# First transfers of the last stage rearranged in a forward and backward kernel of a recurrent-memory transformer block

## Chip, cores, metric

One core of one Trainium2 chip. The metric is the device time of one execution in microseconds (us), as the median of several executions. The kernel before took 3069.97 us (three runs, 3061.94 to 3073.0). In the profile lines PE is TensorE (PEld its weight loads), DVE VectorE, ACT ScalarE, POOL GpSimd and SP SyncE; a "queue" is the list of DMAs that one of these engines issues.

## The reference, cut to what matters

The forward pass is a block with two branches on a layer norm: an attention branch that goes through the sequence in 64 segments of 32 rows and carries 8 memory rows from each segment to the next, and a squared-ReLU MLP. The kernel computes the output and the gradients of ten arguments (`jax.vjp`).

```python
for s in range(n_seg):                       # 64 segments
    h = concat([mem, xs[s]])                 # 8 memory rows + 32 rows, D = 512
    q, k, v = h @ Wq, h @ Wk, h @ Wv         # 32 heads of 128
    p = softmax(mask(q @ k.T * scale))
    o = (p @ v) @ Wo
    mem = o[:M]; outs.append(o[M:])
out = x + concat(outs) + (relu(xn @ w1 + b1)**2 @ w2 + b2)
```

Two stretches matter here. The *recurrence* is the backward pass through the 64 steps, last step first, in 16 blocks of four steps. The *last stage* then computes the weight gradients of Wq, Wk, Wv and Wo, as 16 columns of 160 matmuls each, and the input gradient, 128 rows per column ("input rows").

## The kernel before

The recurrence is written as a list of named operations per step; the kernel plays the list for each block. `L.` marks operations of a block, and `+` or `-` moves an operation by one block or step. The third and fourth row, cut:

```python
B_ORDER = (
    ...
    "... o1te s0 vea L.gs d10 vp1 vla ..."           # third row: L.gs of the block before
    "klb1- o0mm o1mm L.vst o0ev ... vtr ... L.ldt+ ldq- vla d10 L.qtr ... kp0 ldk- ..."   # fourth row
...
o["gs"]  = lambda: dma(S_GM[:, :, b*P:(b+1)*P], gts[b][:])   # store the block's GT
o["ldk"] = lambda: left_of_step(dma, tile_of("kLs", ...), b, j, 1)   # four loads of b_kLs
# dma = SyncE's queue, pdma = GpSimd's queue, nc.scalar.dma_start = ScalarE's queue
```

GT is the gradient that one step hands to the next; DVE writes its last part at the end of the third row. S_GM is its copy in memory, which the last stage reads transposed, as GOc. `qtr` is a DMA transpose, and `ldk` loads b_kLs, which PE reads in the fourth row.

The last stage:

```python
def rows_of(i, g, blocks, left_):            # one column: all in one tile
    t_ = pool.tile([P, RC_ALL, CW], ...)
    q = pdma if i < 2 else dma
    ...
with tc.manual_schedule():
    loads(0)                                 # column 0: GpSimd's queue, 5 MB
    slot_side(GOc, S_GM, gflat)              # 4 DMA transposes + 4 loads, SyncE
    loads(1)                                 # column 1: GpSimd's queue, 5 MB
    slot_side(side, S_HT, S_XN[:])           # HNc, the other operand for Wq, Wk and Wv
for i, (t, g) in enumerate(COLS):            # 16 columns
    loads(i + 2)
    ...                                      # 160 matmuls, evictions, stores on GpSimd's queue
    input_rows(NB - 1 - i)                   # loads, transposes and arithmetic of 128 rows
```

## Time and profile before

| stretch of the profiled execution | us |
|---|---|
| recurrence: end of the first reduction of GT to end of the last | 918.3 |
| from there to the end of the last matmul of the backward pass (ps_m): "last block" | 21.0 |
| first hole: to the first matmul of the last stage | 54.8 |
| last stage: first to last matmul of a weight gradient | 577.6 |
| tail: to the end | 12.4 |

The engines by stretch show start:end, length, then busy us and instructions of PE, PEld, DVE, ACT and POOL, granted clock of PE, DMA share, GB/s.

```profile
1475.71:2394.03 918.32, 829.20 (x21088) 423.37 (x21088) 447.80 (x1278) 332.09 (x945) 352.49 (x683) 0.99 0.70 177
2394.03:2415.04 21.01, 19.20 (x428) 11.04 (x424) 10.65 (x30) 5.81 (x16) 5.93 (x9) 1.00 0.78 261
2469.82:3047.45 577.63, 563.27 (x2622) 258.81 (x2623) 52.78 (x91) 79.79 (x157) 155.35 (x252) 0.98 0.91 188
```

PE is busy for 829 of 918 us in the recurrence: whatever makes PE wait there lengthens the whole. The waits and the chain in the two holes are shown in the prediction.

### The profile page before, as it was taken

How to read it: one execution, taken by the hardware profiler on the slowest of the kernel's cores; microseconds unless marked ns; L12 is line 12 of the kernel's file. 1: busy time of each engine (PE TensorE's matmuls, PEld its weight loads, DVE VectorE, ACT ScalarE, POOL GpSimd, SP SyncE). 2: the span in 40 equal slices, each digit the busy share in tenths (PEclk: the TensorE clock that was granted, in tenths of full speed). 3: DMA queues.
4: the chain of work that ended last, by engine and by line, in shares of the span. 5: the costliest groups of instructions: out<-in, count | busy, mean ns of one | idle time of the engine just before them, and what ended most of it. 6: DMA issues, size and time to landing. Idle time of an engine off the chain costs nothing. (4 is left out here: it accounts for less than half of the span.)

```text
span 3059.8 us, 109712 instructions
## 1 busy us (share of the span) xinstructions
PE 2705.4 (88%) x48600; PEld 1386.8 (45%) x48600; DVE 1319.5 (43%) x3581; ACT 994.7 (33%) x2306; POOL 658.0 (22%) x1264
## 2 busy tenths in 40 slices
PE   8997899999999886877799899998989559999998
PEld 4453444444444444446444444444444224444443
DVE  5452566666666664334345444544545201100010
ACT  2422444444444444323333333333333101111111
POOL 0000000000000000113343433434343213322222
PEclk9998999999999998999999999999999879999999
DMA  9548375766767767777577676776777899898991
GB/s 257 185 146 250 101 188 161 189 181 172 190 168 182 165 157 192 229 230 220 149 173 174 190 187 164 177 203 169 176 200 175 238 192 217 194 211 207 204 207 39
DMA packets 794559, 566.78 MB, mean 185 GB/s; under 512 B 579409, under 2 KB 681570, under 8 KB 790754
## 3 DMA queue, kind: packets, MB, share of 16 engines
q1 hardware_dynamic: 748322, 430.47, 58.8%
q0 software_dynamic: 40528, 126.53, 13.5%
q8 instruction: 381, 6.24, 0.9%
q10 hardware_dynamic: 5232, 2.75, 0.4%
q14 instruction: 96, 0.79, 0.1%
HBM read 193.61 MB, written 238.56 MB: 141 GB/s over the span
## 5 line engine op out<-in xcount | busy, mean ns | idle before, releaser
L1505 PE MATMUL ps_gw<-gn,HNc 128*128 128x512 bf16 x1920 | 416.4, 379 | 0.0
L1505 PEld LDWEIGHTS <-HNc 128*128 128x128 bf16 x1920 | 187.8, 98 | 223.9
L374 ACT CAST f_N<-ps_proj 128x512 bf16<-128x512 f32 x320 | 185.9, 581 | 243.9 <-PE ps_proj L392 223.4
L1476 ACT CAST wt<-ps_gw 128x512 bf16<-128x512 f32 x128 | 74.4, 586 | 503.5 <-PE ps_gw L1505 474.4
L392 PEld LDWEIGHTS <-X 128*32 128x32 bf16 x6144 | 153.3, 97 | 161.3 <-DVE X L482 13.9
L835 POOL COPY kM<-f_kT 128x256 bf16<-128x256 bf16 x64 | 25.6, 401 | 786.7 <-DVE f_kT L377 594.9
L1459 DVE TENSOR_TENSOR gx<-ps_rows,gb 128x512 f32<-128x512 f32 x16 | 11.1, 692 | 420.5 <-PE ps_rows L1457 418.2
L1505 PE MATMUL ps_gw<-GOc,gn 128*128 128x512 bf16 x640 | 142.2, 385 | 54.8 <-DMA GOc<-S_GM 54.8
L460 PE MATMUL ps_gR<-Wk,gk 128*32 128x512 bf16 x2048 | 146.7, 386 | 19.4 <-ACT gk L374 12.9
L392 PE MATMUL ps_proj<-Wk,X 128*32 128x512 bf16 x2048 | 135.4, 384 | 12.6 <-DVE X L482 6.9
L460 PE MATMUL ps_gR<-Wq,gq 128*32 128x512 bf16 x2048 | 141.6, 382 | 1.2 <-issue 1.2
L374 ACT CAST gk<-b_pp 128x256 bf16<-128x256 f32 x192 | 68.8, 377 | 208.3 <-PE b_pp L547 146.6
L1477 POOL DMA_DIRECT2D out_dram<-wt x128 | 69.2, 541 | 309.5 <-ACT wt L1476 309.4
L1239 POOL COPY PD<-b_P 32x320 bf16<-32x320 bf16 x256 | 114.9, 449 | 95.3 <-PE b_pp L1292 64.4
L460 PE MATMUL ps_gR<-Wv,gv 128*32 128x512 bf16 x2048 | 133.4, 379 | 0.3 <-issue 0.3
L392 PE MATMUL ps_proj<-Wo,GT 128*32 128x512 bf16 x2048 | 123.9, 384 | 7.9 <-POOL GT L1203 6.7
L392 PE MATMUL ps_proj<-Wq,X 128*32 128x512 bf16 x2048 | 128.7, 382 | 0.0
L460 PE MATMUL ps_R<-Wo,OT 128*32 128x512 bf16 x2048 | 126.4, 388 | 0.0
L469 PE MATMUL ps_sum<-identF,R 128*128 128x128 f32 x512 | 102.4, 295 | 24.6 <-ACT R L374 18.4
L392 PE MATMUL ps_proj<-Wv,X 128*32 128x512 bf16 x2048 | 124.1, 378 | 0.0
L1505 PEld LDWEIGHTS <-gn 128*128 128x128 bf16 x640 | 63.4, 99 | 132.3 <-issue 59.6
L374 ACT CAST gON<-ps_proj 128x512 bf16<-128x512 f32 x128 | 74.9, 585 | 143.2 <-PE ps_proj L392 141.5
(260 smaller groups left out, 5128.0 us busy)
## 6 DMA issues: line engine op xcount, KB each, us to landing
S_A<-f_N SPq DMA_DIRECT2D x64, 512.0 KB
out_dram<-wt POOLq DMA_DIRECT2D x142, 128.0 KB, 4.6
S_A<-f_N SPq DMA_DIRECT2D x64, 256.0 KB
S_GB<-gv SPq DMA_DIRECT2D x32, 512.0 KB
S_GB<-gq SPq DMA_DIRECT2D x32, 512.0 KB
S_GB<-gk SPq DMA_DIRECT2D x32, 512.0 KB
b_kN<-S_A POOLq DMA_DIRECT2D x63, 256.0 KB, 5.0
b_qN<-S_A POOLq DMA_DIRECT2D x63, 256.0 KB, 5.4
```

Of the source, the lines that this page charges most:

```text
L374: nc.scalar.copy(out, in_)
L392: nc.tensor.matmul(o, lhsT=hT[:, dc, :], rhs=x, start=(dc == 0), stop=(dc == DC - 1), tile_position=(0, 32 * g))
L460: nc.tensor.matmul(o, lhsT=XT(k, g), rhs=x, start=(first and k == 4 * h), stop=(last and k == 4 * h + 3), tile_position=(0, 32 * g))
L469: nc.tensor.transpose(st["T"][:, c * P:(c + 1) * P], R4()[:, c * P:(c + 1) * P], identF[:])
L835: o["km"] = lambda: nc.gpsimd.tensor_copy(B_["kM"][:, :, :, lc], T["kT"][:, :, :, 0:M])
L1239: nc.gpsimd.tensor_copy(PD[32 * g:32 * g + 32, g], C["P"][32 * g:32 * g + 32, :, 0:L])
L1459: nc.vector.tensor_tensor(out=gx[:], in0=ps[:], in1=gb[:], op=ALU.add)
L1476: nc.scalar.copy(wt[:], ps[:])
L1477: pdma(dst, wt[:])
L1505: nc.tensor.matmul(ps[:], lhsT=l(rc), rhs=r(rc), start=(n == 0), stop=(n == RC_ALL - 1))
```

## The change

The intent is to close the hole between recurrence and last stage, and the smaller one behind the first column. GOc's transposes should not share the DMA engines with 10 MB of columns, the stores that they wait for should leave early and from another queue, and the input rows should be there when PE wants them. The core of the diff, shortened:

```diff
-  third row:  "... s0 vea L.gs d10 vp1 ..."       fourth row: "klb1- o0mm o1mm L.vst o0ev ..."
+  third row:  "... s0 vea d10 vp1 ..."            fourth row: "klb1- o0mm o1mm L.gs+ L.vst o0ev ..."
...
+  q = nc.scalar.dma_start if b == 0 and n != "v" and x else dma      # last block's S_GB stores
-  o["sl"] = lambda: dma(S_XGL[b], ...)
+  o["sl"] = lambda: (dma if b > 1 else nc.scalar.dma_start)(S_XGL[b], ...)
-  o["sx"] = lambda: dma(S_XG[b], ...)             # also: the store of gm
+  o["sx"] = lambda: (dma if b > 0 else nc.scalar.dma_start)(S_XG[b], ...)
...
   # a column is now two tiles, gn (16 blocks) and gl (left rows), loaded in parts
-  loads(0)
+  first, second = columns(0), columns(1)
+  for f in first[:2]: f(pdma)                     # 2 MB of column 0 on GpSimd's queue
   slot_side(GOc, S_GM, gflat)
-  loads(1)
+  for f in first[2:] + second: f(dma)             # the rest on SyncE's queue, behind GOc
   slot_side(side, S_HT, S_XN[:])
+  loads(2)
+  load_rows(NB - 1)                               # input rows, one column ahead, on GpSimd's queue
...
-  input_rows(NB - 1 - i)                          # after the last job of a column
+  if k == 3 or i == 0: input_rows(NB - 1 - i)     # after the fourth job
```

The first hunk is written for the last block (the stage's reader waits for that store), but the list is played for every block. A detail that no comment tells: the number `x` of a half is not bound when the store is made, so by the time the four S_GB stores of q and k in the last block are issued it is 2 (a later loop in the same function uses the name again), and all four go on ScalarE's queue.

## The prediction

> **What bounds the kernel now.** I read the page first, then the chain of waits over the last quarter, then the waits of TensorE (PE) there, then the engines by stretch, and last the timeline of single hand-overs. PE is busy 88% of the span; the page's row of slices has one hole (two slices of 5 tenths, 2371 to 2524 us), where the recurrent backward pass ends and the last stage (the weight gradients) begins. The stretches, with PE's busy time as first figure after the length:
>
> ```profile
> 2340.00:2415.00 75.00, 68.56 (x1700) 35.83 (x1692) 37.38 (x107) 24.86 (x73) 28.15 (x52) 1.00 0.73 206
> 2415.00:2470.00 55.00, 0.22 (x2) 0.14 (x2) 1.56 (x5) 0.00 (x0) 4.47 (x7) 0.54 0.93 251
> 2506.00:2521.00 15.00, 0.64 (x4) 0.32 (x3) 0.23 (x1) 3.13 (x6) 8.14 (x16) 0.67 1.11 234
> 2557.00:3048.00 491.00, 490.88 (x2305) 226.43 (x2302) 48.91 (x84) 71.56 (x141) 135.36 (x217) 1.00 0.89 185
> ```
>
> Before 2415 and after 2557 PE is full; between lie two holes, of 55 and 15 us. The waits of PE name them:
>
> ```profile
> PE ps_gw L1505 <- DMA GOc<-S_GM: 54.8, 1, 54.8
> PE ps_rows L1457 <- DVE XT L1448: 14.4, 1, 14.4
> ```
>
> The chain of waits (start, length, what) tells what fills the first:
>
> ```profile
> 2409.55 20.80 DMA gNat<-b_gkL
> 2431.05 16.92 DMA gNat<-b_gvL
> 2448.03 1.31 SPq L1423
> 2449.38 1.31 SPq L1423
> 2451.05 4.79 DMA GOc<-S_GM
> 2456.00 3.06 DMA gNat<-b_gqL
> 2459.07 2.40 SPq L1408
> 2462.04 2.73 SPq L1408
> 2464.82 4.76 DMA GOc<-S_GM
> ```
>
> These are DMA transposes, issued from ScalarE (gNat) and SyncE (GOc), one stream after the other. The same size of transpose (256 KB) takes 20.80 and 16.92 us, then 3.06. During the slow two, GpSimd's queue moves both first columns of gn, 10.5 MB. The packets tell why: in most 5 us slices from 2415 to 2445 the two queues start nearly the same number of packets (440 and 439 from 2435), 4 KB ones of about 160 ns against 256 B ones of about 20 ns. A 256 KB transpose is 64 small packets on each of 16 engines: 64 x 20 ns = 1.3 us alone, 64 x (20 + 160 to 225) ns = 12 to 16 us beside the big ones.
>
> The hand-over that will matter later is one step of the recurrence, SyncE's queue against DVE and PE:
>
> ```profile
> 2320.70 0.56 SPq L1148 DMA_DIRECT2D S_GM<-GT  x1
> 2324.34 0.62 SPq L1190 DMA_DIRECT2D S_GL<-gNat  x1
> 2329.66 1.30 SPq L1247 DMA_TRANSPOSE b_vl<-S_A  x1
> 2331.68 1.24 SPq L1188 DMA_TRANSPOSE gNat<-b_gqL  x1
> 2333.01 1.47 SPq L566 DMA_DIRECT2D b_kLs<-S_NL  x4
> 2335.75 0.29 DVE L482 TENSOR_REDUCE GT<-ps_sum 128x32 bf16<-128x128 f32 x1 [0.53 <-PE ps_sum L469]
> ```
>
> PE reads b_kLs at 2342.09, 6.04 us after that reduction ended. By the landing marks in the trace b_kLs landed at 2340.4: 1.7 us to spare. Over the 14 full blocks the time from reduction to use is 6.03 to 6.21 us and the spare time 0.05 to 3.0 us.
>
> **What the Trainium skill says.** "DMA: Bandwidth & Descriptors", section "Queues, rings and completion order", says that each DMA engine round-robins between queues by the packet; the counts above agree. Its section "Silent corruption: two transposing streams in flight at once" says that transposes of ScalarE and SyncE must wait for each other's completion; the chain shows those waits (SyncE goes on at 2448.03, when gNat<-b_gvL has landed). "Advanced Engine Details and Errata", section "Sequencer Loop", says that control work is done as it is read, so a DMA issue that waits holds up what stands behind it in that queue; the trace agrees: SyncE issues nothing from 2415.4 to 2448.0. "TensorE: Matmul & The Clock Gate", section "What's actually happening", says that an idle PE starts at half clock; here the clock is 0.54 in the hole and the first 160 matmuls take 36.53 us against 34.53.
>
> **The change, part by part.** I built the changed kernel and resolved each wait to the instruction that ends it.
>
> 1. *First hole.* Of the first column only two loads (2 MB) go on GpSimd's queue, and only Wo's last reader, at about 2396, holds them. The rest of column 0 and all of column 1 stand on SyncE behind GOc. ScalarE's queue gets four S_GB stores and S_XG ahead of its transposes. Expected, on the clock of before (ScalarE free at 2409.4): five issues of 0.33 to 0.65 us, so the k transpose issues at 2412.4. The stores are 2048 packets of 1 KB, 128 per engine x 46 ns = 5.9 us, S_XG 0.7, from 2411.5 to 2418.1; the transpose 1.3 us behind them and its landing: 2420.5. The v transpose takes 3.1 (as gNat<-b_gqL did): 2423.6. GOc's first 4.4: 2428. The q transpose 3.1: 2431. GOc's other three 10.5 (2459.07 to 2469.6 before), and 3 us for the input rows of two blocks, 1.6 MB of big packets that GpSimd now loads just then: 2444.5. Gain 2469.8 - 2444.5 = **25.3 us**. Column 0's second half and its left rows (3 MB) are issued by 2450 and needed 14 and 28 us after the start; column 1 (5.2 MB) needs about 15 us at the mean 354 GB/s of 2410 to 2440 and is due 36 us after the start. Both arrive in time. gn for column 2 follows at about 1.6 us a transpose and should be there 5 to 10 us early; I allow **1 us** of loss.
> 2. *Second hole.* The input rows are loaded a job ahead, so their transposes follow the first job at once. From the end of the first job (2506.35) to the second's first matmul (2521.59) were 15.2 us; now an eviction and 1.1 us of ps_rows, about 1.5. Gain **13.7**, and **1.7** more, because PE does not fall to half clock (36.27 against 34.53 us).
> 3. *Tail.* Input rows are worked off in mid-column, so after the last matmul only an eviction and one store remain, not the row arithmetic. The last store was issued at 3056.55; now at 3048.41, as the last weight store was. Gain **8.1**.
>
> ```profile
> 3048.41 0.54 POOL L1477 DMA_DIRECT2D out_dram<-wt  x1 [3.78 <-ACT wt L1476]
> 3056.55 0.58 POOL L1472 DMA_DIRECT2D out_dram<-gi  x1 [2.88 <-issue]
> ```
>
> 4. *The store of S_GM in every block.* Moving it to the head of the block's own last step is meant for the last block, but all 16 get it. Where it stood before it waited for nothing on DVE; now it waits for the reduction of 2336.04, and the S_GL store, the b_vl transpose, b_vTL, the q transpose and the four b_kLs stand behind it. SyncE then runs: S_GM to 2336.7, S_GL to 2337.1, b_vl to 2338.4, b_vTL to 2339.0, the q transpose once S_GL has landed (2339.4) to 2340.7, the last b_kLs issued at 2341.9. A landing takes 2.1 to 2.6 us from there: about 2344.3. PE wants it at 2342.1. So PE stands still about 2.2 us per block. PE has hardly any other idle time here (eleven holes over 0.9 us in 900 us), so nothing absorbs it: 14 x 2.2 = **31 us lost**. In the last block the 2 MB of column 0 (from 2398, 32 big packets per engine) lie beside the q transpose, whose landing and that of b_kLs behind it slip by some 4 us: **6 us**.
>
> Sum: -25.3 - 13.7 - 1.7 - 8.1 = -48.8; +31 + 6 + 1 = +38. From 3070: 3059; as the S_GM term is the softest and some overlap with today's spare time is possible, I say 3057.
>
> **Rivals.** (a) The S_GM move is harmless: then 3070 - 48 = 3022. For it: before, b_kLs waits in rings crowded by GpSimd's b_kN, b_P and b_qN (4 to 6 us to land), and later it would have free rings. Against: the issues alone end at 2341.9 and the spare time is 1.7. (b) It costs 4 us a block, if b_vl and its copy on GpSimd (2340.06 before) become late too, or the rings stay crowded: 3085. (c) The first hole closes further, because the transposes find an empty DMA: at most to some 20 us, for five serial transposes and landings remain; 3048 with the S_GM loss, 3013 without. (d) A new wait opens in the last stage, at columns 1 to 3, since 8 MB and then 36 transposes must follow in one queue while PE runs 36 us a column; SyncE needed 37 us for one column at 2506 beside other traffic. That would give back 5 to 15 us: up to 3072.
>
> **Range and chances.** The gap terms are sure to some 6 us, the block term to 14 x 1.5 = 21 us, the new waits to 8: about 23 together, so an 8-in-10 range of 3028 to 3086. Faster by over 2% is below 3008.6: it needs rival (a) and (c) together and more, 3%. Slower by over 2% is above 3131: over 7 us a block, 3%.
>
> **What would show it.** Right, if PE's wait for GOc<-S_GM is 25 to 33 us and gNat<-b_gkL takes 8 to 10; if the wait of ps_rows is gone and the last store follows the last eviction; if PE waits for b_kLs in each block's last step by about 2 us and the recurrence from 1560 to its end is some 35 us longer. Wrong, if the recurrence has kept its length (then near 3022), if TensorE waits for gn at columns 1 to 3, or if GOc's transposes still find a crowded DMA.

## The result, and the profile after

The changed kernel took **3101.97 us** (four runs, 3096.11 to 3106.75), the kernel before 3068.68 (four runs). The ratio is 1.011, with a 95% interval of 1.0081 to 1.0138. The sign is sure, and 3102 lies above the predicted range (3028 to 3086).

| stretch | before | after | difference | predicted |
|---|---|---|---|---|
| recurrence | 918.3 | 984.5 | +66.2 | +31 |
| last block | 21.0 | 33.8 | +12.8 | +6 |
| first hole | 54.8 | 33.0 | -21.8 | -25.3 |
| last stage (second hole, clock, new waits) | 577.6 | 568.4 | -9.2 | -14.4 |
| tail | 12.4 | 9.7 | -2.7 | -8.1 |
| all before the recurrence | 1475.7 | 1474.6 | -1.1 | 0 |
| span of the profiled execution | 3059.8 | 3104.0 | +44.2 | -10.8 |

The three stretches shown of before, in the changed kernel:

```profile
1474.55:2459.00 984.45, 864.27 (x21088) 434.96 (x21088) 448.34 (x1278) 332.35 (x945) 353.62 (x683) 0.96 0.64 165
2459.00:2492.85 33.85, 21.23 (x429) 11.70 (x424) 10.66 (x30) 5.82 (x16) 1.51 (x2) 0.85 0.69 180
2525.89:3094.32 568.43, 561.18 (x2573) 258.78 (x2624) 55.79 (x94) 79.96 (x159) 151.87 (x243) 0.99 0.98 204
```

The recurrence issues the same 21088 PE instructions. Its idle time (length less PE's busy time) went from 89.1 to 120.2 us, +31.1. That is what the prediction had, though the match to 0.1 us is luck: the waits for b_kLs alone came to 35.6 us in 14 blocks (1.45 to 3.25 us each, but for a few short ones behind them), and other idle time fell by 4.5. But PE's *busy* time grew as well, by 35.1 us, for the same instructions, and the clock went from 0.99 to 0.96.

The waits of PE from the recurrence on (us in total, times, longest):

```profile
PE b_pp L547 <- DMA b_kLs<-S_NL: 46.4, 18, 10.8
PE ps_gw L1528 <- DMA GOc<-S_GM: 33.0, 1, 33.0
```

The first line did not exist before; it holds the blocks' waits and the last block's of 10.8 us. The second is the first hole (54.8 before), and the 14.4 us wait of ps_rows, the second hole, is gone. How a block's wait comes about can be read from SyncE's queue in one block (start, us, operation); the reduction of GT ends at 2266.82:

```profile
2266.85 0.55 SPq L1148 DMA_DIRECT2D S_GM<-GT  x1
2267.45 0.63 SPq L1192 DMA_DIRECT2D S_GL<-gNat  x1
2268.18 1.33 SPq L1249 DMA_TRANSPOSE b_vl<-S_A  x1
2270.38 1.24 SPq L1190 DMA_TRANSPOSE gNat<-b_gqL  x1
2271.71 3.32 SPq L566 DMA_DIRECT2D b_kLs<-S_NL  x4
```

Everything stands behind the store, which stands behind the reduction. In the kernel before (the prediction shows such a block) the last b_kLs load was issued about 1.6 us *before* the reduction ended; here it is issued 8 us after. Between the reduction's end and PE's use lay 6.03 to 6.21 us before and 7.6 to 9.4 us after. What PE does in that block:

```profile
2264.03 1.04 PE L460 MATMUL ps_gR<-Wq,gq 128*32 128x512 bf16 x16
...
2275.97 0.75 PE L547 MATMUL b_pp<-gST,b_kLs 8*128 8x32 bf16 x4 [3.04 <-DMA b_kLs<-S_NL]
...
2276.82 1.90 PE L460 MATMUL ps_gR<-Wv,gv 128*32 128x512 bf16 x16
2278.50 1.92 PE L460 MATMUL ps_gR<-Wk,gk 128*32 128x512 bf16 x16
```

This is the line that the prediction lacks. Sixteen matmuls of the same shape take 1.04 us ahead of the wait and 1.90 and 1.92 us behind it. The trace's clock records agree: in the recurrence the clock was 0.5 for 13.7 us in 3 stretches before and for 81.9 us in 16 stretches after. Each stretch lasts 3.41 or 6.83 us, and but for two of the 16 each begins within 2 us of the end of a wait for b_kLs. At half clock 68.2 us more cost at most 68.2 x (1 - 0.5) = 34 us. PE's busy time leaves 24 to 27 us for it. The matmuls of ps_gR alone are busy for 402.2 instead of 378.0 us (+24.2). Or, from the whole: 35.1 less about 8, because the first group of four late b_kLs matmuls takes 0.75 instead of 0.20 us (each of the four starts some 0.18 us after the one before), in 14 blocks; that is not the clock, since in e4 below such a group takes 0.73 us where the clock is full.

In the last block it is the loads of column 0:

```profile
2461.28 1.51 POOL L1424 DMA_DIRECT2D gn<-S_ON  x2 [5.87 <-PE ps_proj L392]
2463.49 1.45 SPq L566 DMA_DIRECT2D b_kLs<-S_NL  x4
2475.86 0.86 PE L547 MATMUL b_pp<-gST,b_kLs 8*128 8x32 bf16 x4 [10.75 <-DMA b_kLs<-S_NL]
```

GpSimd's two loads of 1 MB are issued just ahead of b_kLs, and PE's use of b_kLs is 12.4 us after its issue instead of the 4.3 of the block shown above. Later in the same block, from 2480 to 2487 us, no queue has anything to move.

The first hole shrank, but its end is slower than it could be (chain of waits; the last line is SyncE issuing GOc's transposes):

```profile
2491.96 5.09 DMA gNat<-b_gkL
2501.05 4.81 DMA GOc<-S_GM
2505.88 3.05 DMA gNat<-b_gqL
2513.99 4.86 SPq L1410
```

gNat<-b_gkL went from 20.80 to 5.09 us, as intended (the prediction had 8 to 10). From the second GOc transpose (2508.95) to the first matmul (2525.89) it takes 16.9 us, where the prediction had 10.5 and 3: GpSimd loads the input rows of two blocks just then, at 2512 to 2520. New waits for gn at column 2 came to 4.2 us. The tail is at the end of the next section.

### The profile page after: what moved, and what is told of

The parts are those of the page before. It is cut to its first block, busy times and chain, and to the rows that moved or that the text cites. A ratio compares the mean times of both kernels' runs of the same rounds, so it can differ in the third digit from the quotient of the medians.

```text
span 3104.0 us, 109562 instructions
## 1 busy us (share of the span) xinstructions
PE 2732.7 (88%) x48451; PEld 1400.1 (45%) x48600; DVE 1320.4 (43%) x3581; ACT 995.1 (32%) x2306; POOL 650.1 (21%) x1250
## 5 line engine op out<-in xcount | busy, mean ns | idle before, releaser
L1528 PE MATMUL ps_gw<-gn,HNc 128*128 128x512 bf16 x1510 | 346.9, 380 | 5.5 <-DMA gn<-S_GB 4.2
L460 PE MATMUL ps_gR<-Wk,gk 128*32 128x512 bf16 x2048 | 156.3, 409 | 19.1 <-ACT gk L374 13.6
L460 PE MATMUL ps_gR<-Wv,gv 128*32 128x512 bf16 x2048 | 146.4, 409 | 0.0
L1528 PE MATMUL ps_gw<-GOc,gn 128*128 128x512 bf16 x501 | 116.0, 384 | 33.9 <-DMA GOc<-S_GM 33.0
L1254 POOL COPY b_vT<-b_vl 128x1024 bf16<-128x1024 bf16 x64 | 67.4, 1053 | 208.0 <-DMA b_vl<-S_A 125.9
```

Of the source, the lines that this page charges most:

```text
L460: nc.tensor.matmul(o, lhsT=XT(k, g), rhs=x, start=(first and k == 4 * h), stop=(last and k == 4 * h + 3), tile_position=(0, 32 * g))
L1254: nc.gpsimd.tensor_copy(vT[:, :, :, 0:SEG], C["vl"][:])
L1528: nc.tensor.matmul(ps[:], lhsT=l(rc), rhs=r(rc), start=(n == 0), stop=(n == RC_ALL - 1))
```

## The experiments

Eleven kernels ran, all correct; "before" is the kernel before in the same rounds. Medians in us:

| run | what | this | before | ratio (95% interval) |
|---|---|---|---|---|
| e1 | early S_GM store in the last block only | 3038.75 | 3066.19 | 0.9907 (0.987-0.9943) |
| e2 | early S_GM store on ScalarE's queue | 3041.93 | 3066.19 | 0.9924 (0.9887-0.9961) |
| e3 | kernel before + the move alone | 3125.65 | 3066.19 | 1.0185 (1.0147-1.0223) |
| e4 | change + 40 unread matmuls in the wait | 3091.23 | 3066.19 | 1.0082 (1.004-1.0123) |
| e5 | e1, first loads of column 0 on SyncE | 3031.85 | 3068.35 | 0.9888 (0.9864-0.9912) |
| e6 | e5, last S_GM store on ScalarE | 3027.43 | 3068.35 | 0.9868 (0.9843-0.9893) |
| e7 | e1, last column's stores on SyncE | 3038.46 | 3068.35 | 0.9904 (0.9875-0.9933) |
| e8 | e6 + e7 + rows and stores rearranged | 3023.5 | 3068.35 | 0.9854 (0.9831-0.9877) |
| e9 | e8, second block of rows back on GpSimd | 3021.52 | 3065.51 | 0.9859 (0.9836-0.9881) |
| e10 | e4 with 16 unread matmuls | 3094.83 | 3065.51 | 1.0092 (1.0077-1.0108) |
| e11 | e8, columns in another order | 3012.65 | 3056.22 | 0.9851 (0.983-0.9873) |

**Theory.** The early store holds SyncE's queue in *every* block; b_kLs lands late, PE waits 2 to 3 us, and each wait drops the clock to half for one or two periods. **Rivals:** another part of the change lowers the clock; the store costs only its waits; the store's traffic and not the hold is to blame.

### e1: the early store in the last block only

```diff
 third row:   + L.gs                fourth row:  - L.gs+   + L.gs0+
+store_gm = lambda: dma(S_GM[...], gts[b][:])
+o["gs"]  = store_gm if b > 0 else lambda: None
+o["gs0"] = store_gm if b == 0 else lambda: None
```

> The changed kernel, but the store of S_GM stands early only in the last block; in the other blocks it is back in its old place. Theory (the early store in every block costs the 66 us that the recurrence grew by): the recurrence from the first reduction of GT to the last goes back from 984 to 918-925 us, the waits for b_kLs are gone but for the last block's of 11 us, the granted clock of the stretch is 0.99 again, and the time is 3102 - 66 = 3036 us (3028 to 3044), below the kernel before. Rival 1 (another part of the change, such as late stores or loads, lowers the clock): the recurrence stays above 950 us and the time above 3070. Rival 2 (the store costs only its waits of 36 us, the lower clock has another cause): 3066.

Measured 3038.75 us (four runs, 3034.41 to 3050.87). The recurrence:

```profile
1470.45:2399.10 928.65, 831.71 (x21088) 426.67 (x21088) 447.81 (x1279) 332.25 (x945) 352.45 (x683) 0.99 0.69 175
```

The waits for b_kLs are gone but for the last block's 9.9 us, and the clock is back at 0.99 (20.5 us at half clock). The profiled execution was the slowest of the four by 8 us, and its recurrence is some us over the 918 to 925 expected. Last block (33.8), hole (33.8) and tail (9.7) are those of the changed kernel. So the move in the fifteen other blocks cost some 62 us (by the ratios, 1.011 against 0.9907), and the rest of the change is worth about 28 us. Rivals 1 and 2 fall.

### e2: early in every block, but on ScalarE's queue

```diff
-o["gs"] = lambda: dma(S_GM[...], gts[b][:])
+o["gs"] = lambda: (dma if b == 0 else nc.scalar.dma_start)(S_GM[...], gts[b][:])
```

> The changed kernel with the store of S_GM as early as the change has it in every block, but issued from ScalarE's queue (SyncE's only in the last block). Theory (what costs is SyncE's queue being held until the reduction of GT ends, with the loads of b_kLs behind it): SyncE runs on as before, b_kLs lands in time, recurrence 918-930 us, time about 3036 (3028 to 3050). Rival 1 (the early store's traffic, not the hold, delays b_kLs): 36 us of waits for b_kLs stay and the time stays at 3090-3105. Rival 2 (ScalarE is as much hurt by the hold as SyncE was): waits of PE for ScalarE's evictions grow by 1 us or more per block, time 3055-3080.

Measured 3041.93 us, recurrence 929.5, clock 0.99; PE uses b_kLs 6.03 to 6.20 us after the reduction in the 14 full blocks, as before.

```profile
1473.92:2403.43 929.51, 837.23 (x21088) 425.46 (x21088) 447.75 (x1278) 332.22 (x945) 352.67 (x683) 0.99 0.69 175
```

The same store, as early and as large, costs nothing that these runs can tell on ScalarE's queue (0.9924 against e1's 0.9907, with intervals that overlap). By the code ScalarE's next work, an eviction of a product of GT, needs that reduction anyway. It is the hold of SyncE's queue, not the traffic.

### e3: the kernel before with the move alone

```diff
 third row:   - L.gs                fourth row:  + L.gs+
```

> The kernel before with nothing but the move of the S_GM store to the head of the block's last step. Theory: the move alone makes the recurrence 60-70 us longer (some 30 us waiting for b_kLs, some 33 us of lower clock), so 3069 + 66 = 3135 us, in 3125 to 3148 (the first hole may shrink by a few us since the last S_GM store is out earlier). Rival (the move hurts only together with the other parts): 3069 to 3085. Rival (only the waits come from the move): 3100 to 3106.

Measured 3125.65 us: +59, at the low end of what was expected (by the 2% rule "unclear", but the interval is clear of 1).

```profile
1473.30:2451.80 978.50, 863.92 (x21088) 434.44 (x21088) 449.24 (x1279) 332.13 (x945) 353.13 (x683) 0.96 0.65 166
```

Recurrence +60.2, of it idle time 114.6 - 89.1 = 25.5 and busy time 34.7; half clock for 78.5 us. Its last block takes 26.0 us instead of 21.0, the first hole is unchanged (54.4). The move does it alone, and costs 5 us in the last block without column 0's loads beside it.

### e4: unread matmuls inside the wait

If the clock falls *because* PE idles, work for PE in the wait must keep it up, though the wait for b_kLs remains.

```diff
 def qp(p=p):
+    if p == 0 and j == 0:
+        for _ in range(40):
+            nc.tensor.matmul(pp(p)[0][:, 0, 4*KW:4*KW+P], lhsT=ident[:], rhs=ident[:],
+                             start=True, stop=True, skip_group_check=True)
```

(The region is overwritten by the real matmuls that follow, so the result stays right.)

> The changed kernel with 40 matmuls of 128x128 that nobody reads put before the matmuls that wait for b_kLs (first half, last step of each block): about 2.1 us of work for PE inside its wait, so that the wait stays but PE idles 0.3-0.9 us instead of 2.5-3. Theory (the halved clock of some 5 us per block follows from PE having idled about 2.5 us): time at low clock in the recurrence falls from 82 to below 25 us, the recurrence from 984 to 950-960 us, the time from 3102 to 3068-3078 although PE does more work. Rival (the lower clock comes from something else, e.g. the load of the chip or this run of the chip): 3100 to 3110 and the clock of the recurrence stays 0.96.

Measured 3091.23 us; half clock in the recurrence for 17.1 us in 5 stretches instead of 81.9 in 16. The same place in a block:

```profile
2260.28 2.39 PE L1306 MATMUL b_pp<-ident 128*128 128x128 bf16 x40 [0.36 <-ACT b_gkL L374]
...
2262.86 0.73 PE L547 MATMUL b_pp<-gST,b_kLs 8*128 8x32 bf16 x4
...
2263.66 1.05 PE L460 MATMUL ps_gR<-Wv,gv 128*32 128x512 bf16 x16
2264.54 1.04 PE L460 MATMUL ps_gR<-Wk,gk 128*32 128x512 bf16 x16
```

The groups of sixteen take 1.05 and 1.04 us again, and the recurrence is 19 us shorter with 600 useless matmuls more in it. So the clock's part is shown to come from PE's idling, by the clock records and the matmuls' lengths of one profiled execution; by the times alone it is not, since the ratios of e4 and of the change (1.0082 and 1.011) have intervals that overlap. All five stretches that remain follow a wait for b_kLs that was still 1.05 to 1.95 us long. The time missed the expected 3068 to 3078: the recurrence went to 965.4, not 950 to 960. The 40 matmuls took 2.39 us, and the mean from reduction to use of b_kLs grew from 8.6 to 9.0 us over the 14 full blocks (6 us in all), so not all of them fitted into the wait.

### e5, e6: the last block's loss

```diff
-for f in first[:2]: f(pdma)
+for f in first[:2]: f(dma)                                      # e5 (on e1)
-store_gm = lambda: dma(S_GM[...], ...)
+store_gm = lambda: (dma if b > 0 else nc.scalar.dma_start)(S_GM[...], ...)   # e6 (on e5)
```

> The run with the early store in the last block only (3039 us), with the first two loads of column 0 on SyncE's queue ahead of GOc's transposes instead of GpSimd's. There they are issued behind the last b_gqL load and S_GL store, at about 2416, into a stretch in which the DMA engines stand idle (2417-2427), not at 2401 beside b_kLs. Theory (in the last block the 2 MB on GpSimd's queue hold up b_kLs): PE's wait for b_kLs falls from 9.9 to 2-4 us, the path from the last reduction of GT to ps_m from 33.8 to 25-27 us (21 in the kernel before, plus the hold of SyncE), the first hole keeps 32-35 us; time 3031 us (3027 to 3035). Rival (b_kLs is late because of the hold and the transposes, not the loads): wait stays at 9-10 and time at 3036-3042.

> As the run before it in this list, and the last block's S_GM store issued from ScalarE's queue too. Theory (what remains of the last block's loss is SyncE held for the reduction of GT): no wait for b_kLs over 1 us, 21-22 us from the last reduction of GT to ps_m as in the kernel before, hole unchanged; time 3026 us (3022 to 3031). Rival (ScalarE then delays its own evictions, or S_GM lands too late for GOc): 3031 or more, with a wait of PE for ScalarE or a longer hole.

e5: 3031.85 us; the wait for b_kLs fell from 9.9 to 2.7 us and the last block from 33.8 to 26.2. e6: 3027.43 us; no wait, 21.0 us as in the kernel before. So of the last block's 12.8 us some 7.6 came from column 0's 2 MB on GpSimd's queue and 5.2 from the hold. The expected hole of 32 to 35 us was missed: 39.3 and 37.4. In e5 the second 1 MB load is issued at 2415.9 and lies beside gNat<-b_gkL, which takes 9 us, and the rows still lie beside GOc's transposes (20.5 and 18.6 us to issue).

### e7: the tail

GpSimd ends the kernel with a drain. In the trace it lasts 2.42 us before (after a store issued at 3056.55, 8 us behind the one before, not the 4 of the expectation below) and 7.49 us after (stores at 3090.96 and 3095.28). The last store itself had landed at 3097.4, 6.5 us ahead of the end; before, it had landed 1.3 us ahead. The last two of the changed kernel:

```profile
3090.96 0.54 POOL L1493 DMA_DIRECT2D out_dram<-wt  x1 [3.78 <-ACT wt L1492]
3095.28 0.54 POOL L1493 DMA_DIRECT2D out_dram<-wt  x1 [3.77 <-ACT wt L1492]
```

```diff
-leave(ps, dst)
+leave(ps, dst, dma if i == len(COLS) - 1 else pdma)
```

> The run with the early store in the last block only (3039 us), with the weight stores of the last column on SyncE's queue instead of GpSimd's. Theory (the tail grew because GpSimd's final drain takes 7.5 us after a DMA that it issued just before, against 2.4 us in the kernel before, where its last store came 4 us after the last one): the drain of GpSimd ends before the last store lands and the tail from PE's last matmul falls from 9.7 to 4.5-5.5 us; time 3034 us (3030 to 3039). Rival (every engine's end costs as much, or the landing sets the end): tail 9-10 us, 3039.

The tail fell from 9.7 to 3.6 us: the drain was what set the end. The time (3038.46) did not fall, since in the profiled execution the first hole was 39.5 us instead of 33.8; the code there is the same, but GOc's transposes took 18.8 us instead of 17.2 and PE then waited for GOc's left rows, again beside the input rows. Why the drain took 2.4 us in one place and 7.5 in the other is open.

### e8: all together, and the rows out of GOc's way

```diff
-def so(n=n, t=t, gs=...)
+def so(n=n, t=t, x=x, gs=...)                # two of the four S_GB stores back on SyncE, earlier
-for f in first[2:] + second: f(dma)
+for f in first[2:]: f(dma)
+load_rows(NB - 1, dma)
+for f in second: f(dma)
+load_rows(NB - 2, dma)
```

> All of the last three together, and: the last block's S_GB halves of q and k that are ready first go on SyncE's queue (in the change all four ended on ScalarE's, because the half's number is read when the store is issued), and the first two blocks of input rows are loaded on SyncE's queue behind column 0's and column 1's loads, not by GpSimd beside GOc's transposes. Expected from the terms: last block 21-22 us, first hole 33.8 to 26-29 us (GOc's transposes take 10.5 us instead of 17.2), waits of column 2 (4.9 us) gone or under 3, tail 5 us: 3039 - 12 - 6 - 3 - 5 = 3013 us (3005 to 3022). Rival (GOc's transposes are slow for another reason than the rows' big packets): hole stays at 32-34 and the time at 3018-3024.

3023.5 us (3019.04 to 3025.53). The first hole is 24.4 us, shorter than in all runs so far, and GOc's transposes issue in 10.33 us, where e6 took 18.59 in the same order of transposes. From the timelines of e6 and of e8, one line each:

```profile
2427.43 18.59 SPq L1412 DMA_TRANSPOSE GOc<-S_GM  x4
```

```profile
2427.93 10.33 SPq L1412 DMA_TRANSPOSE GOc<-S_GM  x4
```

Hole and tail (3.8) came as expected, but not the end of the waits for gn: they rose to 7.9 us, in seven waits at column 2 followed by 13.7 us at half clock, because the rows of the second block now stand ahead of HNc's transposes in SyncE's queue (2462 to 2473). The stage grew to 576.0 us, so the time is above the 3005 to 3022 expected.

### e9, e11: the waits of column 2

```diff
-load_rows(NB - 2, dma)
+gate = p5.tile([P, 1], BF16, ...)
+nc.gpsimd.tensor_copy(gate[:], GOc[:, RC_ALL - 1, 0:1])     # GpSimd waits for GOc
+load_rows(NB - 2)                                           # e9
-COLS = [(3, 0), (3, 1), (2, 0), (2, 1), (2, 2), (3, 2), ...
+COLS = [(3, 0), (3, 1), (3, 2), (2, 0), (2, 1), (2, 2), ... # e11 (on e8)
```

> The combined run (3023.5 us), where PE waits 7.9 us for column 2's gn because SyncE's queue has the second block of input rows (11 us, 2462 to 2473) ahead of HNc's and column 2's transposes. Here that second block goes back to GpSimd's queue, behind a one-element copy that reads the last rows of GOc, so that it cannot start beside GOc's transposes. Theory: column 2's transposes end some 10 us earlier, its waits fall below 1.5 us, the first hole stays at 24-25 us; time 3015 us (3010 to 3019). Rival (the rows on GpSimd slow HNc's transposes by as much as they gave): waits stay at 5-8 us and time at 3020-3025.

> The combined run (3023.5 us) with one thing changed: the third column of the list is one of Wo's (plain loads of 2 KB packets, and no HNc needed), and Wv's first column, which needs HNc and 16 transposes, comes fourth. Theory (what the last stage still loses is that HNc's and the first transposed column's loads stand late in one queue): they are then due 36 us later, PE's waits for gn (7.9 us) fall below 2 us, the stage from first to last matmul goes from 576 to 566-569 us; time 3015 us (3011 to 3019). Rival (each transposed column needs as long as PE needs for one, so the debt only moves to a later column): waits of 5 us or more at a later column, time 3020-3024.

e9's theory fell: 3021.52 us, waits for gn 8.7 us. HNc's transposes began 24 us after the stage's first matmul instead of 33, but took 22.7 instead of 14.4 us beside the rows, as the rival had it. In e11 the stage went from 576.0 to 568.6 us and the waits from 8.5 to 5.3 us (one of 4.7 at Wv's first column, now the fourth), so both theory and rival had a part. By the ratios e8, e9 and e11 can't be told apart (0.9854, 0.9859, 0.9851); each is some 1.5% faster than the kernel before and 2.5% faster than the changed one.

### e10: how much idling drops the clock

```diff
-for _ in range(40):
+for _ in range(16):
```

> The changed kernel with 16 instead of 40 unread matmuls of 128x128 in the wait for b_kLs (about 0.9 us instead of 2.3). In the traces so far the low clock follows exactly those grid windows of 3.41 us in which PE idled over about 1.7 us (lowest that did 1.73, highest that did not 1.69, without filler). Theory (half a window idle is the threshold): the 15 stalls' windows idled 1.75 to 2.91 us in the changed kernel; less 0.9, some 4 to 8 of them remain above the threshold, so 20 to 45 us at low clock in the recurrence (82 without filler, 17 with 40); recurrence 955 to 972 us against 984.5, time 3075 to 3092. Rival (any stall of a microsecond or more halves the clock): still 12 or more low stretches, 65 us or more, time 3100. Rival (a stall must empty a whole window): already 0 to 2.

3094.83 us, recurrence 971.3, half clock for 58.0 us in 15 stretches. The time missed, and the sharp threshold fell; in the number of stretches the first rival was right, in their length it was not. They did get shorter (mostly 3.41 instead of 6.83 us), but windows in which PE idled 1.3 to 1.7 us now went low too. The two figures that the expectation starts from left out traces that were there already: in e2 a window with 1.57 us idle had gone low, in e8 one with 1.71 us had not. In the recurrence of all runs without unread matmuls, the lowest idle time in a window ahead of half clock was 1.42 us (e11) and the highest that had no effect 1.71; with unread matmuls 1.11 and 1.26. So neither "any stall of a microsecond" nor "a whole window" holds. Something near half a window is enough, and what decides is not quite the busy time that the profile records; what it is stays open.

## Why the prediction was wrong, point by point

- **Part 4, the S_GM store in every block: mechanism right, size wrong.** The failed step is "So PE stands still about 2.2 us per block ... 14 x 2.2 = 31 us lost". The wait came as described (PE uses b_kLs 8.6 us after the reduction on the mean, 8.3 by the prediction's sum), and the idle time grew by 31.1 us. What failed is to take a block's loss for the length of its wait. The sum left out the clock: around each such wait the same matmuls run at half clock for 3.41 or 6.83 us, 68.2 us more in all, which cost 24 to 27 us and at most 34. It also left out some 8 us in the first late group of b_kLs matmuls. The block's loss is 4.4 to 4.7 us (62 us by the ratios, 66 by the traces, over 14 blocks), not 2.2. The prediction named the clock at the first hole and priced it for the second (1.7 us), but not for short waits. e3 shows the move's cost alone (+59), e1 its absence (-62), e2 that the hold is its cause, e4 that the clock's part follows from the idling.
- **The last block.** "6 us" was 12.8. The mechanism named was right (2 MB beside the transposes and b_kLs), but it slowed them by 7.6 us, on top of a hold of 5.2 (e5, e6).
- **Part 1, first hole.** 25.3 predicted, 21.8 measured. Up to the second GOc transpose the sum was met (16.1 us after ps_m, 16.0 predicted), in part by luck: ScalarE's five issues took 5.3 us instead of 3, and gNat<-b_gkL 5.1 instead of 8.1. The input rows, put down with 3 us, cost about 6 (16.9 us from the second transpose to the first matmul, less 10.5). e6 and e8 show the same with and without them (18.6 and 10.3 us to issue the four transposes; e8 differs in other transfers too).
- **Part 2, second hole.** It closed as predicted. New waits with their low clock took 5 us more than the 1 allowed (the stage gained 9.2 instead of 14.4): rival (d), at its low end.
- **Part 3, tail.** 8.1 predicted, 2.7 measured. The last store did follow the last eviction; but the end was set by GpSimd's drain, which grew from 2.4 to 7.5 us. e7 takes it away (tail 3.6).
- **Rivals.** (b), 4 us a block and 3085, was nearest in size, but gave another reason. (a) fell with e3.

Together: +35.2, +6.8, +3.5, +5.2 and +5.4 us over the predicted terms are 56 us, less 1.1 ahead of the recurrence: the 55 us between the predicted sum (-10.8) and the difference of the two profiled executions (+44.2). The medians differ by 33 only, since the profiled execution of before (3061.6 us) was faster than its median and that of after (3105.8) slower than its own.

## What to carry to other kernels

Before you move a store for the sake of the last iteration, look whether the schedule plays it in all of them, and what stands behind it in that queue; put it on a queue whose next work needs the same data (e2, e6). Price a new wait of PE not only by its length: here stalls of 2 to 3 us in a busy stretch (31 us of idle time in all) cost nearly as much again (24 to 27 us), in matmuls at half clock. And what is loaded "early" should be early only where the DMA engines are free: 2 MB beside b_kLs cost the last block 7.6 us, and moved behind it they took back some 5 us in the hole, until other transfers had made room (e5, e8).

## What the Trainium skill lacked or had wrong

- "TensorE: Matmul & The Clock Gate", section "What's actually happening", gives half clock "after ≥1 idle window (~3.4µs)", and its section "HAM oscillation — how this bites in real kernels" the rule of no idle gaps over about 3.4 us. Here stalls of 1.45 to 3.25 us were enough (81.9 us at half clock in the changed kernel's recurrence), and one window of 3.41 us in which PE idled only 1.42 us went low, while one with 1.71 us did not. The page gives no length under 3 us that would be enough. The free-running window of 3.41 us that the page names agrees: all stretches at half clock begin on one grid of 3.41 us.
- The same page's penalty (section "Terms": time at half clock times one half) gave 34 us here, as an estimate from 68.2 us more; the busy time showed 24 to 27. PE was busy for 74.1 of the 81.9 us at half clock, which explains a part of the difference.
- No page that I found has the microseconds that the drain of GpSimd at the end of a kernel can take: 7.5 us after stores on its queue 4.3 us apart, 2.4 us where they were 8 us apart, and 6 us off the tail when the last stores went on SyncE's queue (e7).
